# A two-branch block on one core: four early F blocks for five, and work of the query stage moved between engines

## The chip, the cores and the metric

The kernel runs on one core of a Trainium2 chip. The metric is the time of one execution in device microseconds (us). Engines are named as in the profile: PE is TensorE's matmul, PEld its weight load, DVE is VectorE, ACT is ScalarE, POOL is GpSimd, SP is SyncE, which here issues DMAs only.

## The reference

`x` has 2048 tokens of 576 channels. It is normalised over the channels, and two branches start from the result. Branch A is linear attention with 32 heads of 18 channels and a learned feature map; branch B is a gated network with 4608 hidden channels (F). The output is `x + A * silu(B)`.

```python
xn = layernorm(x)
q, k, v = heads(xn @ wqkv)
phi(t) = concat(softmax(t @ w_phi), softmax(-(t @ w_phi)))      # per head, 36 wide
kv = phi(k)^T v ;  z = sum over tokens of phi(k)
A = (phi(q) kv / (phi(q) z + 1e-6)) @ wo
B = (silu(xn @ w_gate) * (xn @ w_up)) @ w_down
out = x + A * silu(B)
```

## The kernel before, in words

Every large product is done in parts: each fp32 operand is split into a high part of reduced precision (`fp32r`, a cast by ACT, line 58) and the remainder (a subtraction by DVE, line 59), and a product is high x high + high x low + low x high. The tokens stand transposed in SBUF (`XB`, two halves of 1024 tokens, each in two blocks of 512). F is cut into 36 blocks of 128.

The stages follow one another on TensorE:

- **Normalisation and folded weights**, then the **key and value stage** (lines 295 to 470). It accumulates for each group of seven heads (126 channels; five groups, `GROUPS`) and each sign of the softmax a state matrix, and with a column of ones beside v also the key sums z. The ten states lie in three PSUM banks, `kvp[0..2]`, four, four and two of them.
- **Masked states and key sums** (lines 493 to 515). The z columns are copied to `zc` (line 500, ten copies), a matmul with the identity spreads each over all 128 partitions (line 506), and four copies (line 509) put them in `zb`, a tile of 128 x 1152. DVE multiplies each state with a block-diagonal mask (line 513), and the result is split into `KVH`, `KVL`.
- **Query stage** (lines 522 to 638). Tokens go in tiles of 128, two to a step. `q_tile` (line 559) computes the features: 28 matmuls of 288 columns, maxima and minima per head, two exponentials into `e` (1152 wide), the per-head sums (line 285); then the product `ez = e * zb` (line 568) and its per-head sum (line 570) give the denominator, and `e` is scaled by it (line 577). `numer` (line 580) transposes `e` of two tiles (line 588) and multiplies with the states (line 594); `project` (line 598) multiplies with wo in four pieces of 15 matmuls (line 614), each copied out of the one bank `p` (line 618). A step issues `numer` of the step before, then its own `q_tile`s, then `project` of the step before.
- Beside it, `tails` (line 542), eight times: the last 64 of the 576 channels of four F blocks' gate and up weights come in (`tl`), GpSimd makes four differences, ACT casts the whole to `th`, DVE subtracts (line 552), and twelve DMAs store high, high and remainder to `t_dram`, all from GpSimd's queue (line 555).
- **Early tiles** (`early_tile`, line 113). A block of 128 F channels for 512 tokens: 14 matmuls each of gate and up, of 512 columns, silu by ACT (line 119) and the product by DVE (line 122), stored to `h_dram`. The first `EARLY` = 5 blocks are computed this way, 4 tiles each, 20 in all. Four of them lie in the first stages and one at the end of the key stage; eleven (the rest of blocks 0 and 1, and blocks 2 and 3) are issued after the query stage but may run between its instructions; the last block's four tiles (line 994 on) bridge to the next stage. Below they are called filler and bridge. A tile's matmuls have the name `pe`.
- **Gate/up and down stage** (from line 648 on, 36 units for each of the two halves). A unit of a block that isn't early is `gate_up` (line 727): gate and up of 1024 tokens by seven products in place of eight, each product 7 matmuls of 512 columns (line 706). A unit of an early block loads its h (`stored`, line 719). Between the products, `fill` takes down projections from a queue (matmuls of 288 columns, line 805). Weights of a block are split once in the first half (by ACT and DVE) and stored in `w_dram`, from which the second half reads them.

The order of the work: the program gives each instruction a place, and a planner reorders them on each engine by its own estimate of when each could start; `high_priority` and `issue_after` shift the place. Within an engine, and within SP's queue of DMA issues, the order that comes out is fixed, and an instruction that waits holds up those behind it.

## Time and profile before

| | |
|---|---|
| time, median of 3 runs | 1643.91 us (1643.0 to 1647.03) |
| the profiled execution | 1645.38 us, its span 1643.6 us |
| granted TensorE clock | 0.998 |
| busy DVE / ACT / POOL | 71% / 44% / 40% of the span |
| DMA | 268.47 MB, mean 163 GB/s |

The span runs from the first to the last instruction that the profile has. Matmuls are pipelined: one of 512 columns is listed with about 0.39 us but the next starts some 0.23 us later, so counts and pitches say more of TensorE than busy time. A row of a group reads: line, engine, operation, output <- inputs, shapes, count | busy us, mean ns | idle time before it and what ended that. A row of the waits reads: who <- whom: us in total, times, longest. A row of the timeline reads: start, length, engine, line, operation, and in brackets the idle time before it.

### The profile page before, as it was taken

The numbers are of one execution on the slowest core, as the hardware profiler recorded it, in microseconds if no ns is written. First come the engines' busy times: TensorE is split into PE (matmuls) and PEld (weight loads), VectorE is DVE, ScalarE is ACT, GpSimd is POOL, SyncE is SP. The second block draws the span as 40 slices with busy tenths as digits, with TensorE's granted clock in tenths as the row PEclk, the third lists the DMA queues.
The fourth block names the chain that finished last, engine by engine and source line by source line (L and its number), as shares of the span: only waits on it lengthen the run. The fifth ranks groups of instructions, "written<-read, shape, count | busy, mean of one in ns | idle before, by whom it ended". The sixth has DMA issues, their size and how long they took to land.

```text
span 1643.6 us, 25222 instructions
## 1 busy us (share of the span) xinstructions
PE 1606.3 (98%) x9385; PEld 1428.2 (87%) x9385; DVE 1173.2 (71%) x1733; ACT 723.1 (44%) x1407; POOL 655.0 (40%) x699
## 2 busy tenths in 40 slices
PE   6999999999999999999999999999999999999997
PEld 5899987999987788888888888888888888888886
DVE  7667768989862678788777788825566766666578
ACT  5533344454432554454444444445433433333334
POOL 3385661433213455355445365313243324133132
PEclk9999999999999999999999999999999999999999
DMA  9522243433239545555545554685454655555445
GB/s 293 197 79 78 88 133 114 119 109 110 79 108 329 183 162 172 182 171 177 174 167 181 178 176 156 222 299 157 134 159 138 199 183 172 168 180 182 139 114 173
DMA packets 121741, 268.47 MB, mean 163 GB/s; under 512 B 12786, under 2 KB 53362, under 8 KB 119826
## 3 DMA queue, kind: packets, MB, share of 16 engines
q1 hardware_dynamic: 106652, 246.49, 45.8%
q0 software_dynamic: 3072, 11.02, 2.5%
q10 hardware_dynamic: 11894, 9.35, 1.8%
q8 instruction: 74, 1.21, 0.3%
q14 instruction: 49, 0.40, 0.1%
HBM read 167.19 MB, written 99.61 MB: 162 GB/s over the span
## 4 chain that ended last, share of the span: by engine, by line
PE 66%; DVE 2%; DMA 1%; issue 1%; POOL 0%; ACT 0%; SPq 0%; DVEq 0%; ACTq 0%
PE pd L805 24%; PE px L706 24%; PE pw L706 12%; PE py L706 6%; PE pe L92 1%; DVE acc L777 0%; DVE w L59 0%; DMA rb<-in_B_w_down 0%; DMA ld<-in_B_w_gu 0%; DVE hh L59 0%; DMA X<-s_dram 0%; DVE dw L59 0%; DVE ha L766 0%; DVE acc L778 0%; DVE s L740 0%
## 5 line engine op out<-in xcount | busy, mean ns | idle before, releaser
L805 PEld LDWEIGHTS pd<-dw,hh 128*128 128x128 f32 x3048 | 433.6, 189 | 25.5 <-DVE dw L59 2.0
L805 PE MATMUL pd<-dw,hh 128*128 128x288 f32 x3048 | 449.7, 297 | 3.2 <-DVE dw L59 1.5
L706 PE MATMUL px<-X,w 128*128 128x512 f32 x1488 | 385.9, 393 | 2.1 <-ACT w L58 1.3
L706 PEld LDWEIGHTS px<-X,w 128*128 128x128 f32 x1488 | 270.2, 188 | 55.5 <-ACT s L735 4.0
L706 PE MATMUL pw<-X,w 128*128 128x512 f32 x744 | 191.8, 393 | 0.0
L706 PEld LDWEIGHTS pw<-X,w 128*128 128x128 f32 x744 | 139.1, 188 | 31.2 <-DVE s L740 0.3
L740 DVE TENSOR_TENSOR s<-pw,s 128x512 f32<-128x512 f32 x124 | 85.3, 688 | 103.2 <-ACT s L735 91.7
L930 DVE TENSOR_TENSOR acc<-pd,acc 128x576 f32<-128x576 f32 x128 | 96.3, 753 | 85.3 <-PE pd L805 85.1
L735 ACT COPY s<-px 128x512 f32<-128x512 f32 x124 | 72.6, 586 | 160.0 <-PE px L706 159.9
L92 PE MATMUL pe<-X,wh 128*128 128x512 f32 (+1 forms) x380 | 121.4, 401 | 5.3 <-ACT h L119 2.2
L58 ACT CAST hh<-ha 128x512 fp32r<-128x512 f32 x140 | 82.7, 619 | 92.9 <-PE pd L805 72.6
L59 DVE TENSOR_TENSOR hh<-ha,hh 128x512 fp32r<-128x512 f32 x140 | 109.9, 811 | 18.1 <-ACT hh L58 17.1
L902 POOL TENSOR_TENSOR hb<-hb 128x512 f32<-128x512 f32 x34 | 46.7, 1372 | 161.9 <-DVE hb L762 161.5
L59 DVE TENSOR_TENSOR w<-ld,w 128x512 fp32r<-128x512 f32 (+1 forms) x93 | 79.6, 858 | 37.6 <-ACT w L58 36.3
L706 PE MATMUL py<-X,w 128*128 128x512 f32 x372 | 97.7, 396 | 1.1 <-ACT py L747 1.1
L706 PE MATMUL px<-X,wt 96*128 96x512 f32 x248 | 97.9, 395 | 0.0
L915 POOL TENSOR_TENSOR ha<-ha 128x512 f32<-128x512 f32 x34 | 52.6, 1563 | 104.0 <-DVE hh L59 104.0
L889 POOL TENSOR_TENSOR h<-ha,hb 128x512 f32<-128x512 f32 x34 | 44.9, 1321 | 123.2 <-DVE ha L766 90.1
L58 ACT CAST w<-ld 128x512 fp32r<-128x512 f32 (+1 forms) x93 | 50.9, 549 | 90.1 <-POOL ld L696 58.0
L92 PEld LDWEIGHTS pe<-X,wh 128*128 128x128 f32 (+1 forms) x380 | 69.9, 189 | 20.6 <-DVE h L122 3.4
L693 POOL TENSOR_TENSOR ts<-ld 128x256 f32<-128x256 f32 x31 | 27.3, 880 | 140.7 <-issue 70.0
L747 ACT COPY py<-px 128x512 f32<-128x512 f32 x62 | 35.5, 572 | 103.7 <-PE px L706 84.4
(262 smaller groups left out, 3238.1 us busy)
## 6 DMA issues: line engine op xcount, KB each, us to landing
w_dram<-w SPq DMA_DIRECT2D x90, 512.0 KB, 2.9
w<-w_dram SPq DMA_DIRECT2D x90, 512.0 KB, 4.5
wt<-t_dram SPq DMA_DIRECT2D x61, 336.0 KB, 3.6
ld<-in_B_w_gu SPq DMA_DIRECT2D x31, 512.0 KB, 4.5
X<-sum_dram SPq DMA_DIRECT2D x8, 1280.0 KB, 11.4
rt<-in_B_w_down SPq DMA_DIRECT2D x33, 288.0 KB, 3.0
rb<-in_B_w_down SPq DMA_DIRECT2D x33, 288.0 KB, 4.3
w_dram<-w SPq DMA_DIRECT2D x30, 256.0 KB, 2.2
```

Source lines behind the costliest of these rows:

```text
L58: nc.scalar.copy(hi, src)
L59: nc.vector.tensor_sub(lo, src, hi)
L92: last = nc.tensor.matmul(ps, l, r, start=n == 0, stop=n == len(pairs) - 1)
L706: nc.tensor.matmul(ps, l, r, start=first and n == 0, stop=last and n == len(mm) - 1, skip_group_check=True)
L735: nc.scalar.copy(t, ps)
L740: nc.vector.tensor_add(t, ps, t)
L747: nc.scalar.copy(yp, xp)
L805: nc.tensor.matmul(ps, l, r, start=first and n == 0 and m == 0, stop=n == len(hs) - 1 and m == 2, skip_group_check=True)
L889: sub(s, g["h"][0][0], g["h"][0][1])
L902: nc.gpsimd.tensor_add(a21, a21, g["h"][1][1])
L915: sub(a12, a12, g["h"][0][0])
L930: nc.vector.tensor_add(a2, pd[:, :, 0:HALF], a2)
```

## The change

It does five things.

1. `EARLY` is 4. Block 4 becomes an ordinary unit in each half; block 3 is the bridge, and seven tiles of filler remain. The number of tail batches stays eight.
2. The key sums and masked states are handled by bank: three `zc` copies, the ten spreading matmuls into three PSUM banks in the order of the groups, two `zb` copies; the mask product and the split go over a whole bank (four, four and two states) at once.
3. `ez = e * zb` is computed by GpSimd, in two halves of 576 columns (two buffers), and DVE sums each half on its own.
4. The remainder of the tails is subtracted by GpSimd.
5. The two stores of the tails' high part are issued by SyncE; those of the remainder stay on GpSimd.

```diff
-EARLY = 5
+EARLY = 4
...
-            for i in range(3):
-                for j in range(4 if i < 2 else 2):
-                    w = GROUPS[(4 * i + j) // 2][1]
-                    nc.scalar.copy(zc[0:w, 4 * i + j:4 * i + j + 1], kvp[i][0:w, j, w:w + 1])
-            for s in range(2):
-                for a, m, name in ((0, 4, ("p2", "vw")[s]), (4, 1, ("vy", "vx")[s])):
...
-                    nc.scalar.copy(zb[:, s * D + o:s * D + o + m * w], zp[:, 0:m * w])
-            for i in range(2 * NG):
-                o, w = GROUPS[i // 2]
-                km = qc.tile([GW, GW], F32, name="km", bufs=2)
...
+            banks = [(i, 4 if i < 2 else 2, GROUPS[2 * i][1]) for i in range(3)]
+            for i, n, w in banks:
+                nc.scalar.copy(zc[0:w, 4 * i:4 * i + n], kvp[i][0:w, 0:n, w])
+            zp, zq = kps.tile([P, 2, 512], F32, name="p2"), kps.tile([P, 512], F32, name="vw")
+            for g, (o, w) in enumerate(GROUPS):
+                for s in range(2):
+                    d = zp[:, s, o:o + w] if g < NG - 1 else zq[:, s * w:s * w + w]
+                    nc.tensor.matmul(d, zc[0:w, 2 * g + s:2 * g + s + 1].to_broadcast([w, P]), ident[0:w, 0:w],
+                                     start=True, stop=True)
+            z2, o = zb.rearrange("p (s n) -> p s n", s=2), GROUPS[-1][0]
+            nc.scalar.copy(z2[:, :, 0:o], zp[:, :, 0:o])
+            nc.scalar.copy(z2[:, :, o:D], zq[:, 0:2 * (D - o)].rearrange("p (s n) -> p s n", s=2))
+            for i, n, w in banks:
+                km = qc.tile([GW, 4, GW], F32, name="km")
+                nc.vector.tensor_mul(km[0:w, 0:n, 0:w], kvp[i][0:w, 0:n, 0:w],
+                                     m4[0:w, 0:w].unsqueeze(1).to_broadcast([w, n, w]))
+                split(KVH[0:w, 4 * i:4 * i + n, 0:w], KVL[0:w, 4 * i:4 * i + n, 0:w], km[0:w, 0:n, 0:w])
...
-                nc.vector.tensor_sub(t, t, hi)
+                sub(t, t, hi)
                 for b, src in enumerate((hi.bitcast(F32), hi.bitcast(F32), t)):
                     for q in range(4):
-                        nc.gpsimd.dma_start(t_dram[n, q, b], src[32 * q:32 * q + 32])
+                        (nc.sync, nc.sync, nc.gpsimd)[b].dma_start(t_dram[n, q, b], src[32 * q:32 * q + 32])
...
-                ez = qk.tile([P, 2 * D], F32, name="ez", bufs=1)
-                nc.vector.tensor_mul(ez, e, zb)
                 y = qk.tile([P, 2 * H], F32, name="y")
-                nc.vector.reduce_sum(y, heads(ez), axis=AX.X)
+                for s in range(2):
+                    ez = qk.tile([P, D], F32, name="ez", bufs=2)
+                    nc.gpsimd.tensor_mul(ez, e[:, s * D:(s + 1) * D], zb[:, s * D:(s + 1) * D])
+                    nc.vector.reduce_sum(y[:, s * H:(s + 1) * H], heads(ez), axis=AX.X)
```

More of the change, by code (lines that the diff above doesn't have):

```diff
@@ L510, in gated_hedgehog_kernel @@
-            for i in range(2 * NG):
-                o, w = GROUPS[i // 2]
-                km = qc.tile([GW, GW], F32, name="km", bufs=2)
-                nc.vector.tensor_mul(km[0:w, 0:w], kvp[i // 4][0:w, i % 4, 0:w],
-                                     mask.rearrange("p h d -> p (h d)")[0:w, 0:w])
-                split(KVH[0:w, i, 0:w], KVL[0:w, i, 0:w], km[0:w, 0:w])
+            zc = qc.tile([GW, 12], F32, name="zc")
+            m4 = mask.rearrange("p h d -> p (h d)")
+            banks = [(i, 4 if i < 2 else 2, GROUPS[2 * i][1]) for i in range(3)]
```

9 lines of the change are left out of this document (1 added, 8 removed).

## The prediction, made before the result was known

> **What bounds the kernel now.** I read the page first (busy times, then the chain that ended last), then the stage windows, then the chain in order of time, and last the waits and single instructions of the stage that the change touches.
>
> ```profile
> PE 1606.3 (98%) x9385; PEld 1428.2 (87%) x9385; DVE 1173.2 (71%) x1733; ACT 723.1 (44%) x1407; POOL 655.0 (40%) x699
> PE 66%; DVE 2%; DMA 1%; issue 1%; POOL 0%; ACT 0%; SPq 0%; DVEq 0%; ACTq 0%
> ```
>
> TensorE is busy for 98% of the span and is nearly the whole chain. A busy PE hides small gaps, though, so I look at the stages. The query stage with its bridge (the fifth early block) lies between 231 and 513 us; the columns are length, then busy time and instructions of PE, PEld, DVE, ACT, POOL, then clock, DMA share and GB/s.
>
> ```profile
> 231.00:275.00 44.00, 40.09 (x210) 33.87 (x210) 34.29 (x58) 22.21 (x30) 15.27 (x23) 1.00 0.49 157
> 275.00:480.00 205.00, 204.99 (x1395) 187.17 (x1393) 180.50 (x279) 92.23 (x164) 55.72 (x112) 1.00 0.31 90
> 231.00:513.00 282.00, 276.65 (x1750) 246.54 (x1750) 221.77 (x347) 121.25 (x208) 80.27 (x146) 1.00 0.41 127
> 560.00:1643.00 1083.00, 1074.14 (x5902) 946.55 (x5900) 760.25 (x1087) 477.67 (x936) 419.67 (x372) 1.00 0.54 174
> ```
>
> In the loop (275 to 480) PE has no idle time that shows, and DVE is second with 180.5 of 205 us, 88%. In the gate/up stage (from 560) PE is busy for 99% and DVE for 70%. So PE sets the pace in both places, with DVE close behind it in the first. The same windows for the early tiles (`pe`) alone, the filler:
>
> ```profile
> 231.00:275.00 44.00, 28.13 (x115) 21.30 (x115) 2.75 (x4) 2.39 (x4) 1.00 0.49 157
> 275.00:480.00 205.00, 56.85 (x196) 34.04 (x196) 4.84 (x7) 4.19 (x7) 1.00 0.31 90
> 231.00:513.00 282.00, 111.45 (x420) 75.64 (x420) 9.72 (x15) 8.97 (x15) 1.00 0.41 127
> ```
>
> There are 420 `pe` matmuls, 15 tiles of 28: eleven of filler and four of bridge. The start-up, which waits for wo and for the first softmax, takes 115 of them; the loop 196.
>
> **The price of one matmul** is its pitch, not its duration. From runs of the chain, and then from the timeline (start, length, count):
>
> ```profile
> 496.22 16.63 PE pe L92 x70
> 688.83 4.80 PE pd L805 x36
> 1221.93 1.63 PE px L706 x7
> ```
> ```profile
> 470.38 1.04 PE L588 MATMUL pt<-ident,e 128*126 128x128 f32 x8
> 471.18 0.38 PE L614 MATMUL p<-WOH,oh 126*128 126x288 f32 x1
> ...
> 471.81 0.40 PE L594 MATMUL po<-ph,KVL 126*126 126x256 f32 x2
> 472.05 0.40 PE L594 MATMUL po<-pl,KVH 126*126 126x256 f32 x2
> ```
>
> That is 0.238 us for a `pe`, 0.133 for 288 columns, 0.233 for a gate/up product's matmul, 0.118 for `po` (two every 0.24), and 0.10 for a transpose (the matmul behind eight of them starts 0.80 us after the first). The query stage's own work by the code is 16x28 + 32x15 = 928 matmuls of 288 columns (123.7 us), 240 `po` (28.3) and 160 transposes (16): 168 us. With 420 x 0.238 = 100 us of `pe` that makes 268 of the 282 us. PE loses some 14 us in the stage. Without filler it would stand at 168 us, below DVE; that is why the filler and DVE's work have to be cut together.
>
> **Term A, the block that moves.** One F block of early tiles is 4x28 = 112 matmuls: 26.6 us leave the query stage. In the gate/up stage the same block is two units of 7x7 = 98 matmuls: 22.8 us come in. Net **-3.8 us**. Down projections are the same 3048. With the block go the stores and loads of its h; one more weight set is written and read back instead, beside a DMA share of 0.54. What its units add for the other engines is the like of
>
> ```profile
> L58 ACT CAST w<-ld 128x512 fp32r<-128x512 f32 x62 | 38.4, 620 | 32.0 <-PE pw L706 13.4 <-ACT py L751 11.3 <-DMA ld<-in_B_w_gu 5.1
> L59 DVE TENSOR_TENSOR w<-ld,w 128x512 fp32r<-128x512 f32 x62 | 55.4, 894 | 13.3 <-ACT w L58 12.8
> ```
>
> four such splits, in a stage where DVE is busy for 70%. I cost them at nothing, since PE's 99% hides them; with that cover gone a split would be 0.62 + 0.89 = 1.5 us, so I keep +2 us as A's other bound.
>
> **Term B, masked states and key sums.** Timeline rows from the last state product to the first query matmul:
>
> ```profile
> 225.25 2.18 PE L295 MATMUL kvp<-v,phi 128*126 128x127 f32 x20
> 226.33 0.35 ACT L500 COPY zc<-kvp 126x1 f32<-126x1 f32 x4 [3.24 <-PE kvp L295]
> 227.70 0.23 ACT L500 COPY zc<-kvp 72x1 f32<-72x1 f32 x2
> 230.50 0.22 ACT L509 COPY zb<-vx 128x72 f32<-128x72 f32 x1
> 230.77 0.40 PE L92 MATMUL p<-QH,X 128*128 128x288 f32 x1 [1.11 <-ACT zb L509]
> ```
> ```profile
> L195 ACT CAST X<-tp 128x1024 fp32r<-128x1024 f32 x8 | 7.9, 1010 | 4.1 <-PE tp L193 4.1
> ```
>
> PE waits for the fourth `zb` copy. Now ten `zc` copies become three (all out by about 227.1), the broadcast matmuls follow bank by bank (done by 228.1), and two `zb` copies remain: 1008 elements, 1.0 us by the row of 1024, and 144 elements, about 0.25. The first query matmul would come near 229.4, 1.4 us earlier; a state cast by bank may slip in front, so I take **-1.2 us**, bounds -1.4 and 0. The mask products and splits by bank only relieve DVE and ACT, and nothing needs them before the first `po`, near 276.
>
> **Term C, DVE to GpSimd.** Groups by line:
>
> ```profile
> L568 DVE TENSOR_TENSOR ez<-e,zb 128x1152 f32<-128x1152 f32 x16 | 21.3, 1331 | 0.0
> L552 DVE TENSOR_TENSOR tl<-tl,th 128x896 f32<-128x896 f32 x8 | 8.6, 1080 | 0.0
> L555 POOL DMA_DIRECT2D t_dram<-th x64 | 31.6, 501 | 42.7 <-ACT th L551 37.2 <-ACT oh L58 4.6 <-issue 0.2
> L251 POOL TENSOR_TENSOR KVWL<-wst,KVWH 128x576 fp32r<-128x576 f32 x4 | 6.1, 1542 | 5.0 <-ACT KVWH L249 4.9
> L778 POOL TENSOR_TENSOR acc<-acc,X 128x576 f32<-128x576 f32 x3 | 5.7, 1897 | 11.9 <-DVE acc L777 9.7 <-issue 2.2
> L122 DVE TENSOR_TENSOR h<-pe,h 128x512 f32<-128x512 f32 x19 | 13.1, 689 | 23.5 <-PE pe L92 15.0 <-issue 3.7 <-ACT e L282 3.0
> L577 DVE TENSOR_TENSOR e<-e,sm 128x1152 f32<-128x1152 f32 x16 | 21.7, 1355 | 0.3
> L547 POOL TENSOR_TENSOR tl<-tl 128x128 f32<-128x128 f32 x8 | 4.8, 603 | 12.1 <-DMA h_dram<-h 10.5 <-DMA tl<-in_B_w_tail 1.5
> ```
>
> DVE gives up 21.3 + 8.6 = 29.9 us, and the four `h` products, 2.8 us. Counted all in the loop, its 180.5 fall to 148, and the loop by 26.6 to 178: 83% instead of 88%. So PE should still set the pace. GpSimd takes on 32 products of 576 columns: the same shape costs 1.54 to 1.90 us there; I take 1.54, the row met in an ordinary stage, so 49 us. The remainder of 896 columns is 896/576 of that, 2.4 us, eight times 19 us. It loses 64 issues, 32 us. From 80 it goes to about 117 of 255 us, 46%, and has room. After the second exponential a tile now needs two products already begun and half a sum, where it had a product of 1.33 us and a whole sum behind the first sum; undisturbed, its chain gets no longer.
>
> The 64 stores go to SyncE. An issue there is shown by
>
> ```profile
> 221.33 0.36 SPq L329 DMA_DIRECT2D sum_dram<-shi  x1
> ```
>
> so 2.9 us for the eight of a batch. They wait for ACT's `th`, and behind them in SyncE's queue stand the raw weights of the next filler block and the h stores. Other tiles of filler stand ahead of these: I take nothing, at most one batch of 2.9 us.
>
> I take C's effect on the lost 14 us as **0**. Better: the 3.9 us that PE idles in the first 44 us go, as ez no longer stands in DVE's way. Worse: the rivals below.
>
> **A rule against this change.** The timeline shows two DVE additions of one shape, and a GpSimd one beside the second:
>
> ```profile
> 1605.48 1.35 DVE L951 TENSOR_TENSOR X<-X 128x1152 f32<-128x1152 f32 x1
> 1609.97 2.68 POOL L953 TENSOR_TENSOR X<-X,acc 128x1152 f32<-128x1152 f32 x1 [12.36 <-DVE sx L952]
> 1610.48 3.39 DVE L954 TENSOR_TENSOR acc<-sx,acc 128x1152 f32<-128x1152 f32 x1
> ```
>
> The second took 3.39 us for 1.35: it stood until GpSimd ended, 2.17 us after its start, then ran. So a DVE product of two SBUF tiles and a GpSimd one exclude each other. The sixteen `e` products (L577) are of that kind. GpSimd's SBUF work will fill 49 + 19 + 19 (the 32 tail differences at 0.60) = 87 of 255 us, a third. Met by chance, half a product of 1.54 us a third of the time, that is 0.25 us x 16 = 4 us on DVE: 85% of the loop. Met always, 25 us.
> The Trainium skill (SBUF — State Buffer, Who interferes with whom) states it as an exclusive lock on a shared pair of ports, held for the whole instruction; L954 agrees.
>
> **Sum.** A -3.8, B -1.2, C 0: -5.0 us. The profiled execution took 1645.38 us with a span of 1643.6, so 1640.4; the median of the runs is 1643.91, 1.5 lower, so **1638.9 us**.
>
> **Rivals.**
> *Better*: the start-up's 3.9 us go too, 1635. For it: DVE is 78% busy there and has the two `ez` products in the first chain. Against: WO's splits and the weights' arrival stay. Chance 0.12.
> *Nothing comes of it*: with 112 matmuls less to put between, the waits that filler hides open up. The waits of the weight loads show which:
>
> ```profile
> PEld p L614 <- ACT so L618: 5.8, 18, 1.8
> PEld p L614 <- ACT oh L58: 4.8, 17, 0.4
> ```
>
> 32 projections wait for a copy of 0.4 us out of a single bank. If a third more of this 10.6 us shows, 3.5 us, the sum is -1.5: 1642.4. This is also the case that the change doesn't do what it says, since a block is only moved. Against: query matmuls can stand between as well. Chance 0.18.
> *Slower*: GpSimd comes late with the products. In front of a product can stand a batch of tails (four differences 2.4, remainder 2.4, four issues 2.0: 6.8 us), or DVE's `e` product by the lock, and the delayed sum then holds up transposes that TensorE has in a fixed order. Price: one product of 1.54 us per tile in the open, 16 x 1.54 = 24.6, less 5.0: 1663.5. In half of the tiles: 1651.2. It takes the gain away from 3.2 tiles on, and makes the kernel slower by over 0.3% from 6.4. For it: DVE at 85% and GpSimd at 46% are one chain then. Against: between a tile's softmax and its transposes lie a projection of 60 matmuls (8.0 us) and the filler. Chance 0.20.
> The forecast has the remaining 0.50.
>
> **The numbers.** A measurement of this kernel can tell about 0.3%, 4.9 us, from no change, so the forecast lies at that edge: of its 0.50 I count 0.38 as faster (any small better start-up puts it over) and 0.12 as the same. Faster 0.38 + 0.12 = 0.50, same 0.12 + 0.18 = 0.30, slower 0.20. The range runs from 1631 (better start-up, and as much again from waits that go with DVE's relief) to 1652 (half of the slower rival); the forecast's own is 1634 to 1642.
>
> **What would show it.** A: `pe` in 231 to the bridge's end 308 instead of 420, gate/up matmuls 3136 instead of 3038 (without the one opening product), and a first gate/up matmul about 28 us earlier than 512.85, where the run of 70 `pe` ends. B: the wait of the first query matmul under 0.5 us and its start near 229.5. C: `ez` at 1.5 to 1.6 us on GpSimd, L577's line still near 1355 ns on the mean, and no wait of transposes or exponentials for GpSimd above 3 us in total. The prediction is wrong if the first gate/up matmul moves by less than 20 us (the stage wasn't bound by PE), or if the stretch from there to the end grows by much more than 23 us.

## The result, and the profile after

| | before | after |
|---|---|---|
| median | 1643.56 us (4 runs, 1643.0 to 1647.03) | 1663.65 us (4 runs, 1662.12 to 1663.77) |
| profiled span | 1643.6 us | 1661.9 us |

The changed kernel is slower: the ratio is 1.0116, with a 95% interval of 1.0098 to 1.0133. The prediction, 1638.9 us and a range up to 1652, missed on the wrong side.

The page of the kernel after, its busy times and its chain that ended last:

```profile
PE 1610.5 (97%) x9371; PEld 1432.6 (86%) x9371; DVE 1164.6 (70%) x1715; ACT 720.8 (43%) x1395; POOL 691.8 (42%) x679
PE 86%; DVE 6%; DMA 3%; issue 2%; POOL 1%; ACT 1%; SPq 0%; ACTq 0%; POOLq 0%; DVEq 0%
```

The two chains can't be compared. The one of the kernel before, in the prediction, adds up to 70% only, because it goes back no further than its first piece (start, length, what):

```profile
496.18 0.04 issue
```

So it holds the end of the bridge and the gate/up stage and nothing of the loop; the one after adds up to 99%. The same windows as before, all engines (length; busy time and instructions of PE, PEld, DVE, ACT, POOL; clock; DMA share; GB/s):

```profile
231.00:275.00 44.00, 33.77 (x172) 29.34 (x171) 31.50 (x42) 21.17 (x26) 26.59 (x30) 0.88 0.52 157
275.00:480.00 205.00, 194.74 (x1327) 178.01 (x1326) 165.81 (x270) 83.79 (x155) 76.95 (x83) 0.98 0.30 88
231.00:513.00 282.00, 258.91 (x1638) 232.01 (x1637) 205.55 (x323) 111.84 (x195) 112.90 (x123) 0.96 0.40 120
560.00:1643.00 1083.00, 1081.86 (x5905) 951.69 (x5904) 752.38 (x1079) 475.11 (x933) 415.71 (x372) 1.00 0.54 174
```

and of those the early tiles alone, then the first gate/up matmul in the timeline:

```profile
231.00:513.00 282.00, 83.90 (x308) 56.38 (x308) 7.54 (x11) 6.58 (x11) 0.96 0.40 120
```
```profile
511.42 0.40 PE L744 MATMUL py<-X,w 128*128 128x512 f32 x1
```

There are 308 `pe` matmuls instead of 420, as forecast, and DVE is busy for 205.6 us of the stage instead of 221.8. Yet the first gate/up matmul starts at 511.42, only 1.3 us earlier than before (512.68; the prediction's 512.85 is where the last `pe` ends), not 28. That is the prediction's own sign that PE didn't bind the stage. Most of the time that the block left behind has turned into idle time: PE is busy for 258.9 of 282 us, not 276.7. From 511.42 to the end come 1150.5 us instead of 1130.9, 19.6 more for the 98 matmuls that came in. **The block was paid for in gate/up, and the query stage gave nothing back.** The gate/up stage itself keeps PE busy as before (1081.9 of 1083 us).

What PE and DVE waited for in the stage, from 231 to 511 us (us in total, times, longest):

```profile
PE p L92 <- DVE e L279: 11.3, 2, 10.2
PE pt L588 <- DVE e L577: 7.8, 8, 3.6
```
```profile
DVE y L570 <- POOL ez L569: 16.4, 11, 5.7
```

DVE's sums wait 16.4 us for GpSimd's products. I had allowed 3 us, but for transposes and exponentials; the transposes (`pt`) wait 7.8 us for DVE's scaling product behind those sums, where the kernel before has 1.3. The longest wait of PE, 10.2 us, lies in the start-up. The timelines of GpSimd, DVE and PE show how it comes about:

```profile
249.52 0.46 POOL L546 TENSOR_TENSOR tl<-tl 128x128 f32<-128x128 f32 x1 [7.44 <-DMA tl<-in_B_w_tail]
...
251.42 1.40 POOL L569 TENSOR_TENSOR ez<-e,zb 128x576 f32<-128x576 f32 x1
...
254.14 2.06 POOL L551 TENSOR_TENSOR tl<-tl,th 128x896 f32<-128x896 f32 x1
...
258.72 1.41 POOL L569 TENSOR_TENSOR ez<-e,zb 128x576 f32<-128x576 f32 x1
```
```profile
252.86 0.75 DVE L570 TENSOR_REDUCE y<-ez 128x32 f32<-128x576 f32 x1 [5.74 <-POOL ez L569]
...
254.19 2.10 DVE L571 TENSOR_TENSOR y<-y,sm 128x64 f32<-128x64 f32 x1
...
258.02 2.17 DVE L573 SCALAR_TENSOR_TENSOR den<-y 128x32 f32<-128x32 f32 x1
260.11 0.74 DVE L279 TENSOR_TENSOR e<-p,m 128x576 f32<-128x576 f32 x1
```
```profile
261.00 0.58 PE L92 MATMUL p<-QH,X 128*128 128x288 f32 x1 [10.23 <-DVE e L279]
```

GpSimd stood 7.4 us in front of a tail difference whose data had not come; the product behind it ran at 251.42, DVE's sum at 252.86. Then two DVE operations of 64 and 32 columns took 2.1 us each, one beside the tails' remainder (L551), one beside a product (258.72). So the subtraction that frees the PSUM bank (L279) ended at 260.85, and the next tile's first matmul had to wait for it.

For the experiments I cut the stretch from the first query matmul to the first gate/up matmul into three: start-up (to the first transposes), loop (to the last projection's last matmul), bridge (to gate/up). "Lost" is the stretch less the matmuls by their pitch (0.235 us a `pe`, 0.133 for 288 columns, 0.118 a `po`, 0.098 a transpose). All numbers are worked out from the timelines of the profiled executions. The first query matmul stands between 228.2 and 241.2 us, so the parts are compared and not the places:

| kernel | start-up (`pe`) | loop (`pe`) | bridge (`pe`) | stretch | lost | gate/up to end |
|---|---|---|---|---|---|---|
| before | 40.2 (104) | 216.9 (212) | 24.8 (104) | 281.9 | 15.7 | 1130.9 |
| after | 37.9 (61) | 220.7 (169) | 22.8 (78) | 281.5 | 41.5 | 1150.5 |
| early4 | 39.7 (104) | 223.4 (204) | 4.3 (0) | 267.4 | 27.5 | 1157.4 |
| hold4 | 39.7 (104) | 210.0 (92) | 27.2 (112) | 276.9 | 36.9 | 1152.1 |
| paced | 30.8 (61) | 233.1 (198) | 16.8 (49) | 280.7 | 40.8 | 1151.3 |
| no_ez | 40.5 (100) | 219.4 (208) | 4.6 (0) | 264.5 | 24.6 | 1157.7 |
| no_tails | 33.7 (61) | 217.3 (195) | 16.9 (52) | 267.9 | 28.0 | 1155.0 |
| no_early | 38.0 (61) | 228.6 (198) | 37.8 (161) | 304.4 | 38.2 | 1127.4 |
| ez | 32.5 (58) | 219.4 (198) | 38.5 (164) | 290.4 | 24.2 | 1128.7 |
| tails | 40.8 (100) | 220.7 (222) | 23.0 (98) | 284.6 | 18.4 | 1128.9 |
| banks | 40.5 (104) | 216.4 (212) | 24.9 (104) | 281.7 | 15.5 | 1128.9 |
| banks_e6 | 40.7 (104) | 217.0 (214) | 50.7 (214) | 308.4 | 16.0 | 1105.1 |
| fill | 42.2 (104) | 215.9 (216) | 24.3 (100) | 282.4 | 16.2 | 1128.3 |
| fill_ez | 34.1 (58) | 233.1 (250) | 26.4 (112) | 293.6 | 27.4 | 1128.3 |
| fill_all | 34.2 (61) | 237.4 (257) | 25.2 (102) | 296.9 | 30.7 | 1128.6 |
| dummy | 42.1 (104) | 219.7 (212) | 24.8 (104) | 286.6 | 20.4 | 1128.4 |
| bare | 35.7 (0) | 202.4 (0) | 27.7 (112) | 265.9 | 72.0 | 1128.6 |
| bare_ez | 16.0 (0) | 229.8 (0) | 30.8 (112) | 276.6 | 82.6 | 1128.7 |
| light5 | 31.5 (53) | 226.0 (255) | 26.4 (112) | 283.9 | 17.7 | 1128.1 |
| light4 | 31.7 (53) | 214.3 (143) | 31.0 (112) | 277.1 | 37.2 | 1149.8 |

### The profile page after: what moved, and what is told of

Its sections match the earlier page's. It is cut to its first block, busy times and chain, and to the rows that moved or that the text cites. A ratio compares the mean times of both kernels' runs of the same rounds, so it can differ in the third digit from the quotient of the medians.

```text
span 1661.9 us, 25224 instructions
## 1 busy us (share of the span) xinstructions
PE 1610.5 (97%) x9371; PEld 1432.6 (86%) x9371; DVE 1164.6 (70%) x1715; ACT 720.8 (43%) x1395; POOL 691.8 (42%) x679
## 4 chain that ended last, share of the span: by engine, by line
PE 86%; DVE 6%; DMA 3%; issue 2%; POOL 1%; ACT 1%; SPq 0%; ACTq 0%; POOLq 0%; DVEq 0%
PE px L706 25%; PE pd L805 24%; PE pw L706 12%; PE py L706 6%; PE p L92 6%; PE pe L92 3%; PE kvp L295 2%; PE p L614 2%; PE vx L383 1%; PE po L594 1%; PE pt L588 1%; DVE e L577 1%; PE tp L193 1%; POOL ez L569 1%; PE vw L383 1%
## 5 line engine op out<-in xcount | busy, mean ns | idle before, releaser
L805 PE MATMUL pd<-dw,hh 128*128 128x288 f32 x3048 | 449.5, 297 | 3.2 <-DVE dw L59 1.5
L706 PE MATMUL px<-X,w 128*128 128x512 f32 x1536 | 398.3, 394 | 1.7 <-ACT w L58 1.0
L706 PEld LDWEIGHTS px<-X,w 128*128 128x128 f32 x1536 | 279.0, 188 | 57.2 <-ACT s L735 4.4
L706 PE MATMUL pw<-X,w 128*128 128x512 f32 x768 | 198.3, 393 | 0.0
L706 PEld LDWEIGHTS pw<-X,w 128*128 128x128 f32 x768 | 143.5, 189 | 32.2 <-DVE s L740 0.3
L92 PE MATMUL pe<-X,wh 128*128 128x512 f32 x300 | 97.9, 405 | 5.0 <-ACT h L119 3.9
L569 POOL TENSOR_TENSOR ez<-e,zb 128x576 f32<-128x576 f32 x32 | 48.2, 1511 | 85.8 <-ACT e L282 78.9
L92 PE MATMUL p<-QH,X 128*128 128x288 f32 (+1 forms) x320 | 69.3, 310 | 11.6 <-DVE e L279 11.3
```

The costliest lines, as they stand in the source:

```text
L92: last = nc.tensor.matmul(ps, l, r, start=n == 0, stop=n == len(pairs) - 1)
L569: nc.gpsimd.tensor_mul(ez, e[:, s * D:(s + 1) * D], zb[:, s * D:(s + 1) * D])
L706: nc.tensor.matmul(ps, l, r, start=first and n == 0, stop=last and n == len(mm) - 1, skip_group_check=True)
L805: nc.tensor.matmul(ps, l, r, start=first and n == 0 and m == 0, stop=n == len(hs) - 1 and m == 2, skip_group_check=True)
```

## The experiments

Each result is the median time, then the ratio to the kernel before, measured beside it, with its 95% interval.

The theories, by the letters that the expectations use. About the block: **F** or **S**, the filler lies in waits of the stage's own chain, and the waits stay when it goes; **B**, only the bridge's early start costs; **D**, DVE's work sets the step once the filler is gone. About the products: **Q**, they stand behind the tails in GpSimd's queue; **L**, GpSimd's use of SBUF stops DVE; **O**, the planner's order leaves filler behind the loop; **C**, the chain through GpSimd is longer.

### One part alone, or one part undone

**early4**: only the number of blocks.

```diff
-EARLY = 5
+EARLY = 4
```

> The kernel before with EARLY = 4 alone. Theory Q (GpSimd's queue: the products come late behind the tails' work, and DVE and TensorE wait for them): the block's move is worth about -4 us or, as DVE keeps its products, nothing: 1638 to 1646 us. Theory F (the lack of filler: with 112 matmuls less the query stage's own waits come into the open): most of the loss is here, 1658 to 1664 us.

1655.32 us, 1.0080 (1.0061 to 1.0098), below F's range and far above Q's. The block alone makes the kernel 0.8% slower, where term A said 3.8 us faster. The planner draws the whole bridge into the loop, and then nothing stands in front of gate/up, which waits for the last projection's copy:

```profile
PE py L744 <- ACT so L618: 4.0, 1, 4.0
```

The stretch gets 14.5 us shorter, where the block's matmuls make 26.6, and the time from gate/up to the end gets 26.5 longer. (The profiled execution, 1660.47 us, is the slowest of the four; the others took 1655.1 to 1655.4.)

**no_ez**: the changed kernel with the products back on DVE.

```diff
...
-                for s in range(2):
-                    ez = qk.tile([P, D], F32, name="ez", bufs=2)
-                    nc.gpsimd.tensor_mul(ez, e[:, s * D:(s + 1) * D], zb[:, s * D:(s + 1) * D])
-                    nc.vector.reduce_sum(y[:, s * H:(s + 1) * H], heads(ez), axis=AX.X)
+                ez = qk.tile([P, 2 * D], F32, name="ez", bufs=1)
+                nc.vector.tensor_mul(ez, e, zb)
+                nc.vector.reduce_sum(y, heads(ez), axis=AX.X)
```

> The changed kernel with the key-sum product and its sum back on DVE as before. Theory Q: nearly all of the loss goes, 1637 to 1645 us. Theory F: the loss stays, and DVE has 21 us more, 1660 to 1668 us.

1650.73 us, 1.0046 (1.0031 to 1.0061), between the two ranges: undoing the products gives back 0.7% of the 1.16.

**no_tails**: the changed kernel with the remainder on DVE and all the tails' stores on GpSimd again.

```diff
-                sub(t, t, hi)
+                nc.vector.tensor_sub(t, t, hi)
...
-                        (nc.sync, nc.sync, nc.gpsimd)[b].dma_start(t_dram[n, q, b], src[32 * q:32 * q + 32])
+                        nc.gpsimd.dma_start(t_dram[n, q, b], src[32 * q:32 * q + 32])
```

> The changed kernel with the tails' remainder back on DVE and all tail stores back on GpSimd. Theory Q: the products stand behind 12 issues of 0.5 us a batch in place of a remainder of 2.1 us and 4 issues, so it is no better, 1660 to 1672 us. Theory L (the lock: DVE's products of two SBUF tiles stand while GpSimd reads): 17 us of GpSimd's SBUF work leave the stage, 1655 to 1661 us.

1652.79 us, 1.0051 (1.0034 to 1.0068), faster than either theory had it: this too gives back 0.65%.

**ez**: the kernel before with the products on GpSimd and nothing else (no_ez's diff, the other way round).

> The kernel before with the key-sum product alone on GpSimd, five early blocks. Theory Q: the loss is here, 1655 to 1668 us. Theory F: the filler is there, so it is within 5 us of the kernel before, 1640 to 1648 us.

1652.92 us, 1.0063 (1.0045 to 1.0081), between the two ranges. The products cost by themselves. The stretch loses 8.5 us more than before (24.2 and 15.7): by the same count 3.1 more in the start-up, 5.9 more in the loop, 0.5 less in the bridge. In the start-up GpSimd again stands in front of a tail difference whose data hasn't come, with a product behind it, and PE then waits for DVE's subtraction:

```profile
249.39 0.46 POOL L547 TENSOR_TENSOR tl<-tl 128x128 f32<-128x128 f32 x1 [6.26 <-DMA tl<-in_B_w_tail]
```
```profile
257.03 0.58 PE L92 MATMUL p<-QH,X 128*128 128x288 f32 x1 [5.45 <-DVE e L279]
```

**tails**: the kernel before with the tails' edit and nothing else (no_tails's diff, the other way round).

> The kernel before with the tails' edit alone: remainder on GpSimd, high parts stored by SyncE (five blocks and the key products on DVE as before). Undone in the changed kernel it gave back 10.9 us. Theory Q/L (the tails cost by standing on GpSimd ahead of the key products, or by the lock against them): without key products on GpSimd nothing is late there, so at most 2 us, 1643 to 1646, ratio below 1.0015, and GpSimd's waits in front of DVE stay below 2 us in total. Rival (the tails' edit costs by itself, by DVE's products that wait for the lock while the remainder runs, or by the h stores and weights behind its stores in SyncE's queue): 5 to 11 us, 1649 to 1655, ratio 1.003 to 1.007.

1645.13 us, 1.0000 (0.9989 to 1.0011). By itself the tails' edit is free; it costs only beside the products.

**banks**: the kernel before with masked states and key sums by bank, nothing else.

> The kernel before with the masked states and key sums by bank alone (term B alone; five blocks, key products and tails as before). All theories that hold term B for what it was forecast: the first query matmul 5.5 us after the last state product begins becomes 4.2, and as nothing behind it changes, the whole is 1.2 us shorter: 1642.4 for 1643.6, a ratio of 0.9993, hardly to be told from 1. Rival: the earlier start is lost again in the start-up's wait for wo's weights and the first softmax: the stretch from the first query matmul to the first gate/up matmul grows by 1.3 us, ratio 1.000. Second rival: the longer key-sum bank takes room or time elsewhere: ratio above 1.001.

1642.08 us, 0.9986 (0.9976 to 0.9996): a small gain. The step itself, last state product to first query matmul, took 5.52 us before; here

```profile
224.27 2.18 PE L295 MATMUL kvp<-v,phi 128*126 128x127 f32 x20
228.48 0.38 PE L92 MATMUL p<-QH,X 128*128 128x288 f32 x1
```

4.21 us, 1.31 less, and the stretch behind it is as long as before (281.7 and 281.9). Term B holds.

**no_early**: the changed kernel with `EARLY = 5`.

> The changed kernel with five blocks computed ahead, all else as changed. Theory S (the stage's length is set by the chain through DVE, so a block in it costs the stage only some 5 us while its 98 gate/up matmuls cost 21 us): the block gives back 12 to 16 us, 1648 to 1652, ratio 1.003 to 1.005 over before, with the stretch from the first query matmul to the first gate/up matmul at 287 to 293 and the rest at 1129. By term A as forecast (TensorE sets the stage): 3.8 us slower than the changed kernel, 1667.5, ratio 1.0145.

1662.53 us, 1.0111 (1.0097 to 1.0125): neither theory's number. Giving the block back changes nothing here, because with products and tails on GpSimd the planner's order leaves 161 `pe` for the bridge, 37.8 us at their full price. One block costs 0.8% in the kernel before and nothing beside the other edits, so the parts don't simply add.

### Why the block that leaves frees so little

**hold4**: four blocks, and the bridge's matmuls ordered behind the last projection, so that the planner can't draw them forward. The filler then runs out in the middle of the loop.

```diff
-EARLY = 5
+EARLY = 4
...
-    early_tile(EARLY - 1, 1, parts)
+    with tc.issue_after(held[-1].ins):
+        early_tile(EARLY - 1, 1, parts)
...
```

> The kernel before with EARLY = 4, and the bridge's matmuls pinned behind the last projection on TensorE. Theory S (the loop's length is set by the chain through DVE and not by TensorE's work; the bridge is drawn into the gaps): the stretch from the first query matmul to the first gate/up matmul stays near 282 us in place of falling by 26.6, so 1660 to 1668 us in all. Theory B (only the bridge's early start costs, since it uncovers the next stage): the stretch falls to 255 to 262 us and the whole to 1638 to 1646 us.

1661.74 us, 1.0107 (1.0089 to 1.0126): the costliest form of the block. Until 370 us its order is that of the kernel before; from there on it has no filler. Two views of 376 to 456 us, three steps: the windows of all engines, first of the kernel before, then of hold4, and of hold4 the early tiles alone.

```profile
376.00:456.00 80.00, 80.00 (x552) 74.11 (x551) 71.61 (x108) 36.06 (x63) 23.30 (x48) 1.00 0.32 94
```
```profile
376.00:456.00 80.00, 73.02 (x493) 66.22 (x491) 76.27 (x120) 28.97 (x58) 23.31 (x48) 0.96 0.30 87
```
```profile
376.00:456.00 80.00, 0.00 (x0) 0.00 (x0) 0.00 (x0) 0.00 (x0) 0.96 0.30 87
```

Three steps of hold4, from transposes at 375.9 us to transposes at 455.5, take 79.6 us with no filler at all. Their own matmuls make 61.7 us by the pitch, so 17.9 us are lost, 6.0 a step. The same three of the kernel before, 378.8 to 461.3, take 82.5 us with 83 `pe` (19.5 us) among them, and lose 3.0. **So 14.9 of the 19.5 us of filler came for nothing.** A part of the 17.9 is the clock, which was granted at one half near the end of the third step:

```profile
448.70:455.50 6.80, 6.31 (x27) 5.96 (x26) 6.63 (x10) 1.06 (x2) 0.00 (x0) 0.50 0.13 43
```

The matmuls that start in this window make 3.3 us by the pitch at full clock, so, as an estimate, about as much is lost by the clock. Where the rest goes, the waits of the weight loads show, first the kernel before (379 to 461), then hold4 (376 to 456, its lines from 570 on stand three further down):

```profile
PEld p L614 <- ACT oh L58: 1.6, 6, 0.3
PEld p L614 <- ACT so L618: 1.3, 6, 0.2
```
```profile
PEld p L617 <- ACT so L621: 5.1, 9, 0.8
PEld po L597 <- DVE ol L59: 1.8, 6, 0.5
PEld po L597 <- ACT ph L58: 1.8, 3, 0.6
```

By the pitch, 10.2 of the 17.9 us lost lie between one projection matmul and the next (1.2 us in the kernel before), 3.3 of them in the window of the slow clock. The row of `p` and `so` points to the one bank of `p` and the copy out of it for 5.1 us; no run gives `p` a second bank. The query stage has waits of its own, and the filler was standing in them.

**bare**: no filler in the stage at all (the bridge pinned as in hold4). The eleven filler tiles are left out, and the units that would read their h read other tiles' h, so part of the computation is replaced. **bare_ez**: the same, with the products on GpSimd.

```diff
...
-        for f, halves in [(1, (0,)), (0, (0,))] + [(f, (1, 0)) for f in range(2, EARLY - 1)]:
+        for f, halves in []:
...
```

> The kernel before without any filler in the query stage (eleven tiles left out, so that the early units read other h tiles), the bridge pinned behind the last projection. Theory S: from the first transposes to the last projection it takes 195 to 215 us, against 217 with 212 filler matmuls (50 us) between. If TensorE sets the loop's length: 217 - 50 = 167 to 175 us.

> The same with the key-sum product on GpSimd. If DVE's work sets the loop's length, it is 15 to 25 us shorter than in the run without this edit. If the chain through GpSimd (theory Q, with the lock) sets it, it is no shorter: 0 to 20 us longer.

One run each: 1637.58 and 1645.98 us. In both the planner put other work ahead of the stage (the first query matmul stands at 241.2 and 238.9 us), so I compare only the stretches. In bare the start-up and loop take 238.1 us, against 257.1 before: 316 matmuls, 74 us by their pitch, cost 19. Some of what bare loses is again the clock: it is 0.50 for 37.5 us of the stretch, and the matmuls that start then make 16.2 us by their pitch. The windows from 300 to 400 us, bare and then bare_ez:

```profile
300.00:400.00 100.00, 93.10 (x644) 85.22 (x643) 91.49 (x141) 38.67 (x77) 41.26 (x84) 0.97 0.40 115
```
```profile
300.00:400.00 100.00, 88.64 (x597) 80.90 (x596) 81.51 (x131) 35.34 (x71) 51.57 (x77) 0.95 0.33 86
```

Without filler DVE is the busiest engine beside PE, 91%. With the products on GpSimd it falls to 82%, and the start-up and loop still grow by 7.7 us (245.8): DVE's busy time alone isn't what sets them either.

**banks_e6**: the kernel of banks with `EARLY = 6`, the block's edit turned around.

> The kernel before with the states by bank and six blocks computed ahead: the edit of term A turned around. One block more brings 112 matmuls, 26.6 us, into the query stage and takes 98, 22.8 us, out of gate/up. Theory S, linear (a quarter of each added microsecond of filler shows, as from no filler to eleven tiles): stage +7, rest -21 to -26: 1622 to 1629, ratio 0.990. Theory S with the room at its end (TensorE loses only 15.7 us in the stage of the kernel before, so at most that much of the added 26.6 us can hide): stage +11 to +27, rest -21 to -24: 1630 to 1647, ratio 0.992 to 1.002. Term A as forecast (TensorE sets the stage already): +3.8 -1.2, 1646.2, ratio 1.0016.

1646.4 us, 1.0003 (0.9994 to 1.0012), by the ratios 0.17% above banks. The planner leaves the sixth block whole to the bridge:

```profile
491.00:542.00 51.00, 50.46 (x214) 40.21 (x214) 4.84 (x7) 4.79 (x8) 1.00 0.62 221
```

There its 110 matmuls cost 25.8 us, and gate/up gives back 23.8. In this direction term A's price nearly holds: it is a price for matmuls that stand alone. Whether the loop had room for the block this run doesn't tell, since none of it stood there (214 `pe` in the loop, 212 before). Downwards from five blocks the price doesn't hold.

**light5** and **light4**: is DVE's load the cause of hold4's long steps (D)? Both leave out the key product and its sum, and order the filler as fill does below and the bridge as hold4 does; light4 has four blocks.

```diff
...
-                ez = qk.tile([P, 2 * D], F32, name="ez", bufs=1)
-                nc.vector.tensor_mul(ez, e, zb)
                 y = qk.tile([P, 2 * H], F32, name="y")
-                nc.vector.reduce_sum(y, heads(ez), axis=AX.X)
+                nc.vector.tensor_mul(y, r, zb[:, 0:2 * H])
...
```

> The kernel before with DVE's key product and its sum (1152 columns each, 2.65 us a tile) left out, one product of 64 columns (0.21 us) in their place, so the denominator isn't the reference's; filler issued step by step and the bridge's matmuls ordered behind the last projection. DVE falls from some 25.4 to 20.5 us a step, TensorE has 20.9 us of its own and 6.6 of filler: TensorE binds. Step 27 to 28 us, stage 273 to 281 us, 1634 to 1642. It is the base for the next kernel.

> The same with four blocks, so without filler from the fourth step on, as in the kernel with four blocks and the bridge held back (there the steps without filler took 26.7 us with DVE busy for 95%, and the block's leaving cost 18 us). Theory D (DVE's work sets the step when the filler is gone): with DVE at 20.5 us the steps without filler take 21 to 23 us, the stage loses 18 to 25 us by the block against the kernel beside it, and the whole comes within -4 to +5 us of that kernel, as term A had it. Rival (the step is a chain of waits whatever DVE's load is, or the bank of the projection holds it): the steps stay at 25 to 27 us, the stage loses 5 to 10 us, the whole is 12 to 18 us slower than the kernel beside it.

1645.42 us, 1.0003 (0.9993 to 1.0012), and 1658.87 us, 1.0084 (1.0067 to 1.0101): light4 came out as the rival had it, 13.5 us above light5, which itself missed its 1634 to 1642. The windows from 380 to 450 us, light5 with 57 `pe` in it and then light4 with none:

```profile
380.00:450.00 70.00, 69.97 (x481) 64.52 (x480) 51.36 (x87) 30.35 (x55) 21.20 (x42) 1.00 0.37 109
```
```profile
380.00:450.00 70.00, 65.25 (x470) 60.11 (x468) 55.96 (x97) 25.61 (x54) 17.65 (x36) 1.00 0.26 73
```

DVE is at 80% in light4, and three steps (transposes at 372.8 to 449.5) still take 76.7 us for 64.8 of matmuls: 11.9 us lost at full clock. hold4 lost 17.9, of which 3.3 by the clock. The waits of light4's weight loads are of the same kind:

```profile
PEld p L614 <- ACT so L618: 3.0, 6, 0.7
PEld p L614 <- ACT oh L58: 2.7, 4, 0.8
PEld po L594 <- DVE ol L59: 1.6, 6, 0.5
```

So D falls as the main cause: without filler the projection's and numerator's waits for small copies open, with less work on DVE too. DVE's load may add to it, but 13.5 us against hold4's 18 is no more than the intervals leave open (some 4 us), and the clock takes its part. And light5 says something else: leaving out operations of 39 us (16 x 2.44) on DVE, whose busy time to the last projection falls from 218.2 us in fill (below) to 190.2, moves the time by nothing while the filler is there.

### Why the products on GpSimd cost

**paced**: the changed kernel with each tails batch ordered behind key products in GpSimd's queue, as the remainder on DVE had been behind an `e` product.

```diff
-                with tc.issue_after(last_e[3 * n // 2 + 2].ins):
+                with tc.issue_after(last_z[2 * (3 * n // 2 + 2) + 1].ins):
```

> The changed kernel with each tail batch's GpSimd work pinned behind the second product of the tile behind which the kernel before held the remainder on DVE. Theory Q: the products are no longer behind tails that run ahead, so the first query matmuls' wait of 10 us and most of DVE's 16 us for the products go: 1645 to 1653 us. Theory L (lock alone): the tails still read SBUF beside DVE, so 1658 to 1664 us.

1661.9 us, 1.0100 (1.0083 to 1.0117). The start-up gets 7 us shorter (30.8 us), and the loop 12 us longer, with 29 more `pe` (6.8 us) in it. The start-up loses 5.3 us by the pitch instead of 12.4, the loop 30.4 instead of 24.9. So the standing behind the tails is real in the start-up, but Q's forecast falls: taking it away there doesn't make the whole faster.

**fill**, **fill_ez**, **fill_all**: O. The filler is issued step by step inside the query loop, and each projection is ordered behind its tiles. fill is the kernel before, fill_ez has the products on GpSimd, fill_all is the changed kernel with five blocks.

```diff
...
+                    for _ in range(4 if n == 1 else 1):
+                        pin = next(fl, pin)
+                    with tc.issue_after(pin.ins):
-                    project(order[n - 1], *om, n == S // QS)
+                        project(order[n - 1], *om, n == S // QS)
...
```

> The kernel before with the eleven filler tiles issued step by step inside the query loop (four before the first projection, then one a step) and each step's projection ordered behind them on TensorE. The order is then almost that of the kernel before (320 early-tile matmuls before the last projection, before: 316). A control: both theories 1643 to 1646, ratio within 0.1% of 1. Rival: the pin itself costs, since a projection waits for a tile whose weights come late: over 1648.

> The same pins with the key products on GpSimd: 308 early-tile matmuls before the last projection, where the planner's own order with the products on GpSimd had 256 and left 164 for the bridge, each at its full price. Theory O (the products cost 9.6 us because the planner leaves 60 matmuls, 14 us, of filler behind the loop, not because the chain got longer): the stage is back at 280 to 284 us, 1643 to 1647, ratio below 1.002. Theory C (the chain through GpSimd is longer, or DVE is stopped by GpSimd's use of SBUF, so each step stretches): the loop grows by what the bridge loses, 1650 to 1655, ratio 1.004 to 1.007.

> The changed kernel with five blocks and the same pins (318 early-tile matmuls before the last projection; without pins 259, and 1662.5 us). Theory O: the 59 matmuls, 14 us, come back: 1646 to 1650, ratio 1.001 to 1.003. Theory C: loop longer by what the bridge loses, 1658 to 1664, ratio 1.008 to 1.011. In between, 1651 to 1657: both, and the difference to the pinned kernel with the products alone is what the tails' remainder costs beside the products.

fill 1644.38 us, 1.0001 (0.9990 to 1.0012); fill_ez 1655.35, 1.0065 (1.0040 to 1.0090); fill_all 1657.18, 1.0071 (1.0053 to 1.0090). With the filler in its old place the products cost as much as without the pins: 52 more `pe` in fill_ez's loop than in ez's made it 13.7 us longer, and the bridge 12.1 shorter. O falls for the products. It seems to explain much of what the tails cost beside the products: with the planner's order no_early stands 0.48% above ez, with the pins fill_all only 0.06% above fill_ez (with uncertainties of some 0.2 and 0.3%; no_early and fill_all include the gain of banks).

**dummy**: L alone. DVE's products stay, and GpSimd makes them once more (544 of 576 columns) into a tile that nobody reads.

```diff
+                for s in range(2):
+                    du = qk.tile([P, 544], F32, name="du", bufs=1)
+                    nc.gpsimd.tensor_mul(du, e[:, s * D:s * D + 544], zb[:, s * D:s * D + 544])
```

> The kernel before, key products on DVE as they were, with the same products (544 of the 576 columns) made once more on GpSimd into a tile that nobody reads: GpSimd's use of SBUF without the chain through it. Theory L (the shared SBUF access: with the products on GpSimd DVE's scaling products, their small two-input neighbours and the remainders of the weights took some 10 us longer): DVE stood at 245 of the stage's 257 us, so most of 8 to 10 us shows, 1650 to 1655, ratio 1.004 to 1.007, with the scaling product near 1600 ns instead of 1355. Theory C or O (latency or order): under 2 us, ratio below 1.0015.

1649.76 us, 1.0030 (1.0019 to 1.0041), between the two theories' ranges: GpSimd's use of SBUF alone costs 0.3% where DVE keeps its products. The scaling product overwrites `e`, so in dummy it also has to come behind GpSimd's reading, but the idle time before it is only 1.0 us in all. DVE's groups show where it goes, in the kernel before, in dummy (its lines are three further down) and in ez (one further down), 231 to 513 us:

```profile
L575 DVE TENSOR_TENSOR sm<-sm,den 128x64 f32<-128x64 f32 x16 | 3.5, 216 | 0.3
L63 DVE TENSOR_TENSOR wl<-raw,wh 128x512 fp32r<-128x512 f32 x8 | 5.4, 688 | 6.2 <-ACT wh L62 6.1
```
```profile
L580 DVE TENSOR_TENSOR e<-e,sm 128x1152 f32<-128x1152 f32 x16 | 24.0, 1503 | 1.0
L578 DVE TENSOR_TENSOR sm<-sm,den 128x64 f32<-128x64 f32 x16 | 6.7, 422 | 0.3
L63 DVE TENSOR_TENSOR wl<-raw,wh 128x512 fp32r<-128x512 f32 x8 | 7.5, 953 | 5.6 <-ACT wh L62 5.6
```
```profile
L578 DVE TENSOR_TENSOR e<-e,sm 128x1152 f32<-128x1152 f32 x16 | 25.1, 1567 | 0.2
L576 DVE TENSOR_TENSOR sm<-sm,den 128x64 f32<-128x64 f32 x16 | 8.0, 501 | 0.2
L571 DVE TENSOR_REDUCE y<-ez 128x32 f32<-128x576 f32 x32 | 23.2, 728 | 6.6 <-POOL ez L570 6.5
```

The scaling product goes from 1355 to 1503 and 1567 ns, the product of 64 columns from 216 to 422 and 501, the weights' remainder from 688 to 953. From the first query matmul to 5 us behind the last projection the durations of DVE's operations add up to 237.6 us before, 247.8 in dummy and 228.5 in ez (without the overlap of neighbours, busy for 219.0, 228.7 and 210.5). So of the 21.3 us that DVE gave up in ez, 9.1 are left. What came back are operations with two inputs that took longer beside GpSimd (3.4 in the scaling products, 4.5 in the products of 64 columns, the rest in smaller groups), and 2.1 us more for the sums in halves.

How ez's 0.63% divides isn't shown. dummy's 0.3% comes with DVE busier than before; in ez the same operations get longer but DVE is less busy than before, and light5 says that DVE's load hardly counts there. What ez's trace shows is the start-up's 3.1 us behind a tail difference and 5.9 us more lost in the loop. For those, the longer chain (C) and the shared access (L) are both left; fill_ez shows that it isn't the order of the filler, and no run takes them apart.

## Why the prediction was wrong, point by point

The step that failed is term A's: that the query stage gets shorter by the matmuls that leave it.

- **"TensorE is busy for 98% of the span and is nearly the whole chain."** The chain read there starts at 496.18 us and adds up to 70%, so it couldn't say what sets the pace in the loop. It was taken for evidence on a stage that it doesn't reach.
- **"So PE sets the pace in both places."** Half right. With the filler in place it does: light5, with 39 us less on DVE, is at 1.0003. But that says nothing of what happens when filler goes. PE was at its pitch because filler stood in its waits (against hold4, 14.9 of 19.5 us of it came for nothing).
- **Term A is the step that failed: "26.6 us leave the query stage".** The count was right (308 `pe`), and the price in gate/up nearly so: 19.6 us in the changed kernel, 21.2 in hold4, against 22.8. The matmuls leave, but not their time: the stage gets 5.0 us shorter in hold4 (281.9 to 276.9) and 14.5 in early4, where the bridge is used up as filler and the time from gate/up on grows by 26.5. The lost time rises from 15.7 to 36.9 us in hold4. In the place of -3.8 the block alone gives +0.8% (early4), some 13 us.
- **Term B, -1.2, held**: 1.31 us at its place, and the whole 0.14% shorter (0.04 to 0.24).
- **Term C, "0"**: right for DVE's relief, which is worth nothing here (light5), wrong for its price. DVE was to lose 29.9 us of products and remainders and 2.8 of h products; the durations of its operations fall by 23.4 (237.6 to 214.2). The products alone cost 0.63%. L577 was to stay near 1355 ns and is at 1553 (24.8 us for 16); waits of transposes or exponentials for GpSimd were to stay below 3 us; it is DVE's sums that wait, 16.4 us, and the transposes behind them 7.8. The durations of GpSimd's products, 1.5 us, were right. The SP stores and the remainder were free by themselves (tails, 1.0000), though not beside the products.
- **The rule against the change.** I priced the shared access at 4 us of DVE time, by the sixteen `e` products alone. They lost 3.1 in the changed kernel, near that; but the small products with two SBUF inputs lose as well, and the same exclusion cost some 10 us of DVE time in dummy, where the whole became 0.3% longer. The Trainium skill (SBUF — State Buffer, Who interferes with whom) says that a DVE instruction with two SBUF inputs contends with a GpSimd one that reads SBUF; the 2.10 us of a product of 64 columns beside L551 agree, and the sums (L285, one input) kept their 1348 ns (1345 after), which agrees too.
- **The rival "Slower"** named the right engines and gave 1663.5, which the result hit; its mechanism gives only part of it. Its first reason, a tails batch in front, is what the start-up shows, but pinning it away gained nothing in the whole (paced). Its second, the shared access, costs 0.3% by itself (dummy); its share in the products' 0.63% is open. The block's price, 0.8% alone (early4), that rival did not have at all.
- **The rival "Better"** had the start-up's sign wrong: it loses 12.4 us by the pitch, where the kernel before loses 4.6.
- **The rival "Nothing comes of it"** had the block's mechanism: "the waits that filler hides open up", at the projections' single bank. Its size was wrong: 3.5 us for a block, by a third of the waits that showed *with* filler. Without it hold4 loses 6.0 us a step, and 21 us more in the stretch.
- **How the total comes about.** Each part alone: block +0.80%, products +0.63, tails 0.00, banks -0.14, sum 1.29; together 1.16 (each with an uncertainty of 0.1 to 0.2). Undone one at a time from the changed kernel: products -0.70, tails -0.65, block -0.05. The sum is near the whole, but the parts overlap: beside the other edits a block's worth is near nothing, with much of the filler left behind the loop (no_early), and the tails cost only beside the products.

The best version found is banks alone, 0.14% faster than the kernel before. What stays open is how the products' cost divides between the longer chain through GpSimd and the shared access.

## What to carry to other kernels

A pace-setting engine that is 100% busy may be so because filler stands in the waits of a chain; what filler costs is not its pitch but the difference to the steps without it, and steps with little filler, or a run with it taken out, show that price. A chain of waits says something only of the stages that it reaches; where its shares don't add up to the span, look where it begins. Work moved from DVE to GpSimd should be priced with all of DVE's operations that have two SBUF inputs, the tiny ones first, and with the chain that now crosses another engine's queue. And check whether the relieved engine is worth relieving: a run with its work left out is a cheap bound.

## What the runs showed of the hardware that was not expected

- Tiny DVE operations with two inputs can cost ten times their length beside GpSimd: 2.10 us for 128x64 at 254.19 (mean before 0.21), 2.17 for 128x32 at 258.02 (0.19); both end within 0.1 us of the GpSimd operation beside them (256.20 and 260.13).
- TensorE's granted clock was one half after idle time in this stage. In the changed kernel's window after the 10.2 us wait, then the next:

```profile
261.00:264.60 3.60, 3.60 (x15) 3.60 (x16) 3.60 (x6) 1.86 (x2) 0.00 (x0) 0.50 0.51 152
264.60:268.00 3.40, 3.40 (x22) 3.13 (x20) 3.32 (x4) 0.00 (x0) 1.19 (x1) 0.90 0.35 111
```

  The granted clock is 0.50, and query matmuls follow each other every 0.240 us instead of 0.133 until 265.2: 16 matmuls at 0.107 us too much, 1.7 us on top of the wait. The Trainium skill (TensorE: Matmul & The Clock Gate, What's actually happening) describes such a gate; this case's rows agree with a clock of one half. In the kernel before, whose filler stands in this place, the clock of 231 to 275 us is 1.00, here 0.88. Over the stretch from the first query matmul to gate/up the clock is 0.50 for 20.5 us in the changed kernel, 13.7 in hold4 and not at all in the kernel before. The matmuls that start then make 8.0 and 7.1 us by their pitch, so, as an estimate from these numbers, about a third of the 25.8 and 21.2 us that these kernels lose more is the slow clock. No run holds the clock fixed. A long wait wasn't needed: in the changed kernel's loop the clock was 0.50 after 3.4 us in which PE was busy for 1.81 us and no wait was longer than 1.59:

```profile
296.00:299.40 3.40, 1.81 (x13) 1.54 (x13) 3.40 (x4) 0.00 (x0) 2.37 (x5) 1.00 0.31 72
299.40:302.80 3.40, 3.40 (x15) 3.40 (x16) 3.23 (x8) 0.40 (x1) 0.46 (x1) 0.50 0.65 198
```
